# Windowed attention and a squared-ReLU MLP in one kernel: the scores of a group become one recorded operation, the planner's durations are replaced and a cost for 64/128-row changes is added, and the noise is drawn from one seed per stretch

## Chip, cores and metric

One core of one Trainium2 chip. The metric is the time of one launch in device microseconds. Three runs of the kernel before gave 292.73, 292.80 and 292.94 us (median 292.8). Engines are named as in the profile: PE is TensorE's matmuls, PEld its weight loads, DVE is VectorE, ACT is ScalarE, POOL is GpSimd, SP is SyncE.

## What is computed

```python
# q, k, v: (8, 8, 576, 64) float32; w_in: (512, 2048); w_out: (2048, 512)
scores = matmul(q, k.transpose(0, 1, 3, 2)) / sqrt(64)
scores = where(abs(pos[:, None] - pos[None, :]) <= 32, scores, -1e9)
attn = softmax(scores)
x = matmul(attn, v).transpose(0, 2, 1, 3).reshape(4608, 512)
h = maximum(x @ w_in, 0)
out = (h * h) @ w_out          # (4608, 512) float32
```

## The kernel before

All 4608 tokens pass through one pipeline. **Attention** works in 24 groups of 192 tokens (three to a batch, all 8 heads). Queries and keys of a group are loaded in bf16 by POOL's DMA queue, turned so that the 64 head dimensions lie on partitions (`turn_pe` with identity matmuls for groups 0 to 5, `turn_dma` with SP's DMA transposes after that), and multiplied: the *scores* S. Groups 3 to 23 use `scores_steps` (line 664): 24 matmuls with 64 rows of weights (two heads side by side on 128 partitions), 16 of them (steps 0 and 2, `S{G}A`) into PSUM banks 0 and 1 of the tile `at`, 8 (step 1, `S{G}B`) into banks 2 and 3. ACT takes the exponentials (`X{G}A`, tile `e`, 1024 columns, and `X{G}B`, tile `em`, 512 columns), DVE multiplies by the band mask (`M`, tile `pt`; one of 1024 columns, two of 512 on 64 partitions). Then the products with v, `pv` (line 707): two of 8 matmuls each, `P{G}A` and `P{G}B`, into banks 2 and 3 of `at`, each followed by a reciprocal `R` and a scaling `N` on DVE (tiles `xa`, `xb`); between the two the upper half of the banks is cleared (`Z`). The result is turned into `xt` (`xturn`, line 767): by PE and ACT for groups below `NXT`, by SP's DMA transposes from there on.

**The MLP** takes `xt` in tiles of 192 tokens, from token 2304 on 256 (`mm1`, line 840): calls of 8 matmuls into the banks `ht`, ReLU on ACT (tile `rt`), square on DVE or ACT (tile `gt`). The second product runs for pairs of 128-token blocks (`mm2_pair`, line 913): seven products of 8 matmuls in place of eight, with sums of `gt` blocks (`ss`) and of weights (`tw`) made on DVE; the first two blocks use `mm2`. Results leave over ACT's DMA queue.

**What sets the order.** The code records every operation with its engine, what it reads and writes, a duration and a key (a due time in units of 64 tokens). `Prog.schedule` (line 159) plays the whole program through with these durations and a latency for each engine (`LAT`): whenever an engine is free it takes, of the operations that would be ready, the one with the smallest key. Where an operation has an alternative on another engine (`FLEX`), either may take it. Keys get an offset by kind (`OFFS`) and a random part (`SEED`, `NOISE`). The order so found is written out; on the chip each engine runs its instructions in that order and waits by semaphore. In the opening, matmuls on zeros (line 386) stand where the plan has PE idle. `OPENING` is the order of the first loads, by name: `('k', 2)` are the keys of group 2, `w1` and `w2` quarters of the weights, `('v', 1, 0)` one half of the values of group 1, `hq` and `hk` the first queries and keys over SP's queue.

Of the kernel before, what the change touches and what calls it, by code (L numbers as in the profile page):

```python
# [22 lines left out]
NXT = 6  # L23
LEAD = 8
LAG = 9.0
AHEAD = 14.0
GFAR = 12
GATE = 'P{}B'
GD = 3
GK = 6.5  # L30
TDKEY = 4.5
# [14 lines left out]
NCLR = 1  # L46
# [5 lines left out]
LSLACK1 = 1000  # L52
HOLD = {}
KMIN = 0.5
HOLDT = 26000
# [8 lines left out]
SEED = 12603  # L64
NOISE = 0.2
# [7 lines left out]
OPENING = [('k', 1), ('w1', 0), ('v', 0, 0), ('q', 1), ('v', 0, 1), ('q', 2), ('k', 2), ('v', 1, 0),  # L73
# [6 lines left out]
LAGP = 9.5  # L80
PSTEP = 0.45
SLEAD = 2.0
MOE = 0.5
SQBEG = 576
ULATE = 28
HLATE = 4608
E3 = 576
E3B = 1
OFFS = {'S': 1.5, 'M': -1.0, 'g': -4.75, 'Z': -4.0, 'N': -3.75, 'cc.': 4, 'u': -2.5, 'X': 0.75, 'r': 4, 'c': -0.5}
DLEAD = 0.3  # L90
TWKEY = 5
# [3 lines left out]
FLEX = {'g': 4.75, 'Z': 0.5, 'ev': 4.5, 'o': -1.0, 'p': 3.75}  # L95
# [9 lines left out]
class Prog:  # L105
# [3 lines left out]
    LAT = {"PE": 205, "ACT": 200, "DVE": 30, "POOL": 100, "SP": 0}  # L109
# [40 lines left out]

    def free_order(self, d, op, eng):

        if d.eng == eng == "PE":
            return True
        if d in op.raw or d.dma is not None or op.dma is not None or d.eng != eng:
            return False
        return not (d in op.own and eng in ("ACT", "DVE"))

    def schedule(self):
        ops = self.ops  # L160
        rnd = random.Random(SEED)
# [17 lines left out]
        free["POOL"] = 850  # L179
        wait = {e: [] for e in engs}  # L180
# [46 lines left out]
        while True:  # L227
# [32 lines left out]
            if op.taken:  # L260
                continue
            op.eng, op.lat, op.taken = e, self.LAT[e], True
# [67 lines left out]
def act(n):  # L330
    return 52 + 0.833 * n


def dve(n, fast=True):
    return 156 + (0.525 if fast else 1.042) * n


class Gen:
# [197 lines left out]
    def turn_pe(self, t, b, g, key):  # L536
# [9 lines left out]
        def f(e):  # L546
            for j in range(4):
                for x in range(2):
# [5 lines left out]
                   dur=8 * 52, name=f"turn{t}{b}{g}")  # L554
# [44 lines left out]
    def scores(self, G, ws):  # L599
# [44 lines left out]
        self.moe = self.p.rec("PE", f, reads=rd, writes=[t for w in ws for t in tags[w]], key=key, dur=190 + 235 * len(ws),  # L644
# [19 lines left out]
    def scores_steps(self, G):  # L664
# [21 lines left out]
        self.p.rec("PE", lambda e: f(e, (0, 2)), reads=rd, writes=lo, key=key, dur=SDUR * 2 // 3, name=f"S{G}A")  # L686
# [472 lines left out]
```

## Time and profile before

| | before |
|---|---|
| median of three runs | 292.8 us |
| the profiled execution: its time, its span | 292.72 us, 290.9 us |
| granted TensorE clock | 1.0 in all 40 slices |
| busy, of the span | PE 97%, PEld 85%, ACT 75%, DVE 68%, POOL 37% |
| matmuls: pairs (256 columns) | 952 in 128x256, 273 ns each on the page |
| matmuls: scores of groups 3 to 23 | 504 in 64x64, 191 ns each on the page |

The span runs from the first to the last instruction; the 1.82 us between it and the execution's time lie around it. Matmuls are pipelined: the duration of one on the page (273 ns) is longer than the distance from its start to the next one's, so PE's busy share hides small gaps. Where the time of a piece of PE's work matters, the start of the next piece is subtracted from its own, in the view in order of time.

### The profile page before, as it was taken

How to read it: one execution, taken by the hardware profiler on the slowest of the kernel's cores; microseconds unless marked ns; L12 is line 12 of the kernel's file. 1: busy time of each engine (PE TensorE's matmuls, PEld its weight loads, DVE VectorE, ACT ScalarE, POOL GpSimd, SP SyncE). 2: the span in 40 equal slices, each digit the busy share in tenths (PEclk: the TensorE clock that was granted, in tenths of full speed). 3: DMA queues.
4: the chain of work that ended last, by engine and by line, in shares of the span. 5: the costliest groups of instructions: out<-in, count | busy, mean ns of one | idle time of the engine just before them, and what ended most of it. 6: DMA issues, size and time to landing. Idle time of an engine off the chain costs nothing.

```text
span 290.9 us, 8382 instructions
## 1 busy us (share of the span) xinstructions
PE 283.2 (97%) x3438; PEld 246.2 (85%) x3445; DVE 199.2 (68%) x433; ACT 219.4 (75%) x400; POOL 107.1 (37%) x143
## 2 busy tenths in 40 slices
PE   8898999999999999999999999999999999999996
PEld 3478788699989999999998889889888889888885
DVE  6895677885786888377847685578666877615263
ACT  4498999878858888897978776877778768676710
POOL 8999757731000245606660645216460000000000
PEclk9999999999999999999999999999999999999999
DMA  8999999999999499999999999989999230202024
GB/s 167 177 205 182 199 182 157 159 176 140 175 143 175 104 120 128 187 122 157 111 169 170 154 124 120 216 140 128 127 181 178 47 101 19 74 10 74 0 74 144
DMA packets 158151, 39.39 MB, mean 135 GB/s; under 512 B 147489, under 2 KB 153761, under 8 KB 158113
## 3 DMA queue, kind: packets, MB, share of 16 engines
q0 software_dynamic: 106016, 17.93, 86.5%
q1 hardware_dynamic: 47056, 11.88, 30.2%
q10 hardware_dynamic: 5040, 9.05, 10.2%
q8 instruction: 27, 0.44, 0.7%
q14 instruction: 12, 0.09, 0.1%
HBM read 36.70 MB, written 9.44 MB: 159 GB/s over the span
## 4 chain that ended last, share of the span: by engine, by line
PE 87%; ACT 7%; DVE 3%; DMA 2%; issue 1%; SPq 0%; ACTq 0%; DVEq 0%
PE ht L857 39%; PE outp L943 32%; PE at L943 4%; PE at L678 4%; PE at L731 4%; DMA oe<-in_k_dram 2%; PE outp L883 2%; ACT rt L863 2%; ACT e L655 1%; ACT qt L577 1%; ACT kt L582 1%; PE outp L857 1%; ACT gt L873 1%; DVE kt L580 1%; DVE qraw L493 0%
## 5 line engine op out<-in xcount | busy, mean ns | idle before, releaser
L857 PE MATMUL ht<-xt,w 128*128 128x192 bf16 (+1 forms) x1280 | 139.1, 258 | 0.0
L857 PEld LDWEIGHTS ht<-xt,w 128*128 128x128 bf16 x1280 | 112.8, 98 | 7.8
L863 ACT ACTIVATE rt<-ht 128x384 bf16<-128x384 f32 (+1 forms) x160 | 84.0, 537 | 32.8 <-PE ht L857 24.2
L873 ACT ACTIVATE gt<-rt 128x384 bf16<-128x384 bf16 (+1 forms) x122 | 69.4, 573 | 3.5 <-ACT rt L863 0.2
L507 POOL DMA_DIRECT2D v<-in_v_dram x48 | 38.3, 808 | 23.1 <-PE at L731 16.5
L458 POOL DMA_DIRECT2D kraw<-in_k_dram x36 | 28.1, 785 | 44.6 <-PE at L731 27.7
L458 POOL DMA_DIRECT2D qraw<-in_q_dram x36 | 28.2, 786 | 41.6 <-issue 34.5
L943 PE MATMUL outp<-w,gt 128*128 128x256 bf16 x240 | 31.2, 273 | 0.0
L943 PE MATMUL outp<-tw,gt 128*128 128x256 bf16 x240 | 31.1, 273 | 0.0
L943 PE MATMUL outp<-tw,ss 128*128 128x256 bf16 x240 | 30.6, 273 | 0.0
L871 DVE TENSOR_TENSOR gt<-rt 128x384 bf16<-128x384 bf16 (+1 forms) x46 | 17.2, 378 | 13.0 <-ACT rt L863 12.6
L943 PEld LDWEIGHTS outp<-tw,ss 128*128 128x128 bf16 x240 | 22.9, 98 | 2.6
L943 PEld LDWEIGHTS outp<-tw,gt 128*128 128x128 bf16 x240 | 22.9, 98 | 2.7
L943 PEld LDWEIGHTS outp<-w,gt 128*128 128x128 bf16 x240 | 22.6, 98 | 2.8
L703 DVE TENSOR_TENSOR pt<-em,mask 64x512 bf16<-64x512 bf16 x42 | 17.6, 420 | 8.8 <-ACT em L692 7.7
L689 ACT ACTIVATE e<-at 128x1024 bf16<-128x1024 f32 x21 | 21.5, 1024 | 2.2 <-PE at L678 2.0
L963 DVE TENSOR_TENSOR oe<-outp,uu 128x256 f32<-128x256 f32 (+1 forms) x30 | 16.7, 555 | 8.1 <-PE outp L943 6.9
L731 PE MATMUL at<-v,pt 128*128 128x66 bf16 x384 | 20.1, 194 | 0.5 <-ACT pt L652 0.5
L963 DVE TENSOR_TENSOR uu<-outp,uu 128x256 f32<-128x256 f32 x30 | 12.7, 422 | 10.4 <-PE outp L943 7.1
L731 PEld LDWEIGHTS at<-v,pt 128*128 128x128 bf16 x384 | 17.8, 98 | 1.8 <-ACT pt L652 0.6
L753 DVE TENSOR_TENSOR xa<-at,rs 64x512 bf16<-64x512 f32 x24 | 16.7, 695 | 1.0
L750 DVE RECIPROCAL rs<-at 64x8 f32<-64x8 f32 (+1 forms) x48 | 10.0, 208 | 10.6 <-PE at L731 9.6
(109 smaller groups left out, 324.0 us busy)
## 6 DMA issues: line engine op xcount, KB each, us to landing
out_dram<-oe ACTq DMA_DIRECT2D x34, 256.0 KB, 3.3
qraw<-in_q_dram POOLq DMA_DIRECT2D x36, 96.0 KB, 6.2
w<-in_moe_w_in_dram POOLq DMA_DIRECT2D x4, 512.0 KB, 11.1
v<-in_v_dram POOLq DMA_DIRECT2D x16, 128.0 KB, 7.8
w<-in_moe_w_out_dram POOLq DMA_DIRECT2D x4, 512.0 KB, 18.8
v<-in_v_dram POOLq DMA_DIRECT2D x16, 96.0 KB, 7.4
kraw<-in_k_dram POOLq DMA_DIRECT2D x12, 112.0 KB, 5.4
kraw<-in_k_dram POOLq DMA_DIRECT2D x12, 96.0 KB, 7.0
```

The source lines that it names most:

```text
L458: self.p.rec("POOL", lambda e, j=j: e.dma_start(raw[0:h, j, :].rearrange("p (h d) -> p h d", h=8), s[:, j]), writes=[("raw", t, G % NRAW, ...
L507: self.p.rec("POOL", lambda e, j=j, lo=lo, hi=hi, k0=k0: e.dma_start(vt[lo - k0:hi - k0, j, :, 0:64], self.v[b, :, lo:hi, :].rearrange("h ...
L689: self.p.rec("ACT", lambda e: e.activation(e2[:], self.AT[:, 0:1024], ACTF.Exp, scale=0.125), reads=lo, writes=[("e", n)], key=key, dur=ac ...
L703: self.p.rec("DVE", lambda e, w=w, r=r, x=x, mm=mm: e.tensor_tensor(pt[x:x + 64, w, :, 0:64], e1[r:r + 64, :].rearrange("p (h q) -> p h q" ...
L731: mm = e.matmul(avp[:, c:c + VS], pt[:, 4 * (h % 2) + h // 2, :], vt[:, w, h, :], start=(w == 0 and y == 0), stop=True, skip_group_check=True)
L753: self.p.rec("DVE", lambda e: e.tensor_tensor(x[r0:128, :].rearrange("p (x y c) -> p x y c", x=2, y=4), av[:, :, :, 0:64], rb, ALU.mult), ...
L857: mm = e.matmul(ht[:, n * x:n * x + n], self.W1[:, ft, 128 * d:128 * d + 128], self.XT[:, ft, r:r + n], start=(ft == 0), stop=(ft == 3))
L863: self.p.rec("ACT", lambda e: e.activation(rt[:, 0:c], ht[:, 0:c], ACTF.Relu), reads=htag, writes=[("rt", k % 4)], key=key, dur=act(c), na ...
L871: self.p.rec("DVE", lambda e: e.tensor_tensor(gt[:, d0:d0 + len(ds), r:r + n], rr, rr, ALU.mult), reads=[("rt", k % 4)], writes=wr, key=ke ...
L873: alt=("ACT", lambda e: e.activation(gt[:, d0:d0 + len(ds), r:r + n], rr, ACTF.Square), act(c), "g")
L943: mm = e.matmul(op[:, 256 * half:256 * half + 256], a[:, d, :], w[:, d, :], start=first and d == 0, stop=d == 7, skip_group_check=True)
L963: self.p.rec("DVE", lambda e: e.tensor_tensor(out, src, other, ALU.add), reads=btags[bank] + rd, writes=wr, key=key + k * PSTEP - DLEAD, d ...
```

## The change

`scores_steps` records one PE operation for the 24 score matmuls of a group. It writes all four banks and carries one semaphore count at its end; before, there were two operations with a key each.

```diff
-        self.p.rec("PE", lambda e: f(e, (0, 2)), reads=rd, writes=lo, key=key, dur=SDUR * 2 // 3, name=f"S{G}A")
-        self.moe = self.p.rec("PE", lambda e: f(e, (1,)), reads=rd, writes=hi, key=key + 0.02, dur=SDUR // 3, name=f"S{G}B")
+        if SMERGE:
+            self.moe = self.p.rec("PE", lambda e: f(e, (0, 2, 1)), reads=rd, writes=lo + hi, key=key, dur=350, name=f"S{G}B")
+        else:
...
```

The planner charges PE for a change of kind, and may hold on for a score operation that stands at most `STICK` above the smallest key:

```diff
+    def kind(self, op):
+        n = op.name
+        return "s" if n[0] == "S" or n[0] == "T" and n[-1] == "a" else "t" if n[0] == "t" else "v" if n[0] == "P" and "." not in n else ""
+
+    def change(self, a, b):
+        return 0 if a == b else 110 if b == "s" else 100 if a == "s" or b == "t" else 30 if b == "v" else 0
...
+            if e == "PE":
+                k = self.kind(op)
+                if last == "s" != k:
+                    more = [x for x in pool[e] if not x[2].taken and x[0] < first[0] + STICK and self.kind(x[2]) == "s"]
+                    if more:
+                        heapq.heappush(pool[e], (op.key, op.i, op))
+                        op = min(more)[2]
+                        k = "s"
+                t += self.change(last, k)
+                last = k
```

Durations, latencies and keys:

```diff
-    LAT = {"PE": 205, "ACT": 200, "DVE": 30, "POOL": 100, "SP": 0}
+    LAT = {"PE": 170, "ACT": 150, "DVE": 145, "POOL": 100, "SP": 0}
...
-    return 52 + 0.833 * n
+    return 60 + 0.833 * n
...
-    return 156 + (0.525 if fast else 1.042) * n
+    return (40 if fast else 60) + (0.557 if fast else 1.042) * n
...
-NXT = 6
-LEAD = 8
+NXT = 5
+LEAD = 11.0
...
-GFAR = 12
+GFAR = 10
...
-TDKEY = 4.5
+TDKEY = 3.0
...
-LAGP = 9.5
+LAGP = 7.5
...
-MOE = 0.5
+MOE = -1
...
-ULATE = 28
-HLATE = 4608
+ULATE = 32
+HLATE = 4096
...
-SEED = 12603
-NOISE = 0.2
+SEEDS = (32084, 52688, 82796, 32593, 79449, 14325, 66926, 90467, 77586, 2794, 60200, 19844, 43771, 14133, 3007, 27362, 8058, 26041, 26079, 54464)
+NOISE = 0.8
...
-            n = rnd.uniform(-NOISE, NOISE)
-            if SEED and op.key > -20:
-                op.key += n
+            if op.key > -20:
+                op.key += rnds[min(max(int((op.key + 12) // 5), 0), len(rnds) - 1)].uniform(-NOISE, NOISE)
```

Other durations are replaced in the same way (a reciprocal 117 for 212, a `turn_pe` 250 for 416, a `pv` 222 for 260, a store 420 for 600), and `OFFS`, `FLEX` and `OPENING` have new entries. The matmuls of the two products and of attention are the same in number, but for one group: with `NXT` at 5, group 5 is turned into `xt` by SP's DMA transposes (8 fewer matmuls on PE, one fewer ACT operation, two more transposes on SP). ACT has 12 squares fewer and DVE 12 more.

**PE, group 7, in the steady part.** `at<-qt,kt` are scores, `at<-v,pt` the products P, `ht<-xt,w` calls of `mm1`, `outp<-...` products of a pair. Before:

```order
L678 MATMUL at<-qt,kt 128x64 x16
L857 MATMUL ht<-xt,w 128x192 x16
L678 MATMUL at<-qt,kt 128x64 x8
L943 MATMUL outp<-tw,gt 128x256 x8
L857 MATMUL ht<-xt,w 128x192 x16
L731 MATMUL at<-v,pt 128x66 x8
L943 MATMUL outp<-w,gt 128x256 x8
L943 MATMUL outp<-w,ss 128x256 x8
L943 MATMUL outp<-tw,gt 128x256 x8
L731 MATMUL at<-v,pt 128x66 x8
```

The same group now, up to the scores of group 8:

```order
L697 MATMUL at<-qt,kt 128x64 x24
L879 MATMUL ht<-xt,w 128x192 x16
L965 MATMUL outp<-w,ss 128x256 x8
L879 MATMUL ht<-xt,w 128x192 x8
L753 MATMUL at<-v,pt 128x66 x8
L879 MATMUL ht<-xt,w 128x192 x16
L965 MATMUL outp<-tw,gt 128x256 x8
L753 MATMUL at<-v,pt 128x66 x8
L879 MATMUL ht<-xt,w 128x192 x16
L965 MATMUL outp<-w,gt 128x256 x8
L697 MATMUL at<-qt,kt 128x64 x24
```

The scores moved together. Over the program, the scores of groups 3 to 23 stood in 32 places on PE (11 of 16, 11 of 8 and 10 of 24 matmuls) and stand in 21 of 24 now.

**PE in the opening, from the first `mm1` call to the second scores of group 2.** `outp<-ident,kraw` turns the keys of group 2; `128x64 x8` from `qt,kt` with 128 columns are scores of groups 1 and 2. Before:

```order
L549 MATMUL outp<-ident,kraw 128x80 x8
L630 MATMUL at<-qt,kt 128x128 x8
L731 MATMUL at<-v,pt 128x66 x8
L857 MATMUL ht<-xt,w 128x192 x16
L630 MATMUL at<-qt,kt 128x128 x8
L857 MATMUL outp<-xt,w 128x192 x8
L731 MATMUL at<-v,pt 128x66 x8
L857 MATMUL ht<-xt,w 128x192 x8
L630 MATMUL at<-qt,kt 128x128 x8
```

Now:

```order
L649 MATMUL at<-qt,kt 128x128 x8
L879 MATMUL ht<-xt,w 128x192 x8
L753 MATMUL at<-v,pt 128x66 x8
L879 MATMUL ht<-xt,w 128x192 x8
L879 MATMUL outp<-xt,w 128x192 x8
L879 MATMUL ht<-xt,w 128x192 x8
L753 MATMUL at<-v,pt 128x66 x8
L568 MATMUL outp<-ident,kraw 128x80 x8
L833 MATMUL at<-ident,xa 128x64 x4
L649 MATMUL at<-qt,kt 128x128 x8
L838 MATMUL at<-ident,xb 128x128 x4
```

The keys of group 2 are turned later, and its first scores stand behind four `mm1` calls, not two.

**POOL's loads in the opening**, from the queries of group 1 on (`tw` is the buffer in which the first queries and keys land). Before:

```order
L490 DMA tw<-in_q_dram 96x8x128
L507 DMA v0<-in_v_dram 128x8x64
L490 DMA tw<-in_q_dram 96x8x128
L490 DMA tw<-in_k_dram 80x8x128
L507 DMA v1<-in_v_dram 64x8x64
L507 DMA v1<-in_v_dram 128x8x64
L520 DMA w1<-in_moe_w_in_dram 128x4x512 x3
```

Now:

```order
L509 DMA tw<-in_q_dram 96x8x128
L526 DMA v0<-in_v_dram 128x8x64
L526 DMA v1<-in_v_dram 64x8x64
L509 DMA tw<-in_q_dram 96x8x128
L526 DMA v1<-in_v_dram 128x8x64
L539 DMA w1<-in_moe_w_in_dram 128x4x512
L509 DMA tw<-in_k_dram 80x8x128
```

The keys of group 2 (`80x8x128`) went behind the values of group 1 and a second quarter of `w1`.

More of the change, by code (lines that the diff above doesn't have):

```diff
@@ L160, in schedule @@
         ops = self.ops
-        rnd = random.Random(SEED)
+        rnds = [random.Random(x) for x in SEEDS]
         for op in ops:
@@ L179, in schedule @@
         free["POOL"] = 850
+        last = ""
         wait = {e: [] for e in engs}
@@ L643, in scores @@
             rd += [t for w in ws for t in tags[w]]
-        self.moe = self.p.rec("PE", f, reads=rd, writes=[t for w in ws for t in tags[w]], key=key, dur=190 + 235 * len(ws),
+        self.moe = self.p.rec("PE", f, reads=rd, writes=[t for w in ws for t in tags[w]], key=key, dur=215 * len(ws),
                               name=f"S{G}{'AB'[ws[-1]]}")
@@ L741, in pv @@
             rd += [("pt", G % 2, 0, 0), ("pt", G % 2, 0, 1), ("v", G % NV, 0)]
-        self.p.rec("PE", f, reads=rd + (lo if w and G >= NDUP else []), writes=hi + lo, key=key, dur=260 + 160 * (w and G < NCLR) + 260 * (w and G < NDUP),
+        self.p.rec("PE", f, reads=rd + (lo if w and G >= NDUP else []), writes=hi + lo, key=key, dur=222 + 160 * (w and G < NCLR) + 222 * (w and G < NDUP),
                    name=f"P{G}{'AB'[w]}")
@@ L896, in mm2 @@
             self.p.rec("ACT", lambda e: e.dma_start(self.out[128 * u:128 * u + 128, :], oe),
[L897 removed]
+                       reads=[("oe", u % 4)], writes=[("out", u)], dma=(f"o{u % 4}", u), key=key, dur=420, move=(8, 80), name=f"st{u}")
     def setup_tw(self, key):
```

37 lines of the change are left out of this document (20 added, 17 removed), and 6 rows, old and new, of the table OPENING.

## The prediction, on record before the changed kernel ran

> **What bounds the kernel now.** I read the page's busy times first, then a table of stages, then PE's instructions in order of time.
>
> ```profile
> PE 283.2 (97%) x3438; PEld 246.2 (85%) x3445; DVE 199.2 (68%) x433; ACT 219.4 (75%) x400; POOL 107.1 (37%) x143
> ...
> 0.00:24.00 24.00, 20.17 (x227) 12.44 (x229) 19.38 (x60) 15.79 (x23) 23.03 (x34) 1.00 1.39 183
> 24.00:60.00 36.00, 34.83 (x460) 28.95 (x466) 25.70 (x55) 32.25 (x61) 27.24 (x36) 1.00 1.84 174
> 60.00:288.30 228.30, 228.18 (x2756) 204.78 (x2752) 153.70 (x319) 171.33 (x316) 56.83 (x74) 1.00 1.18 123
> ```
>
> The stage rows give start and end, length, the busy time of PE, PEld, DVE, ACT and POOL, the granted clock, the DMA share and GB/s. From 60 us to the end of the last matmul PE is busy 228.18 of 228.30 us at full clock; ACT has 171 and DVE 154. So in that stage the time is PE's own queue of matmuls and nothing else, and only less work on PE, or work that PE finds late, changes it. Before 24 us PE mostly fills with matmuls on zeros; from 24 to 60 us it loses little.
>
> Busy time is too coarse for the question, because a pipelined matmul lasts longer than its place in the queue. The starts tell it:
>
> ```profile
> 130.89 0.41 PE L678 MATMUL at<-qt,kt 64*128 64x64 bf16 x16
> 131.23 0.43 PE L731 MATMUL at<-v,pt 128*128 128x66 bf16 x8
> 131.50 1.48 PE L857 MATMUL ht<-xt,w 128*128 128x192 bf16 x16
> 132.82 1.04 PE L943 MATMUL outp<-w,gt 128*128 128x256 bf16 x8
> 133.69 1.04 PE L943 MATMUL outp<-tw,ss 128*128 128x256 bf16 x8
> 134.66 0.29 PE L678 MATMUL at<-qt,kt 64*128 64x64 bf16 x8
> 134.88 1.49 PE L857 MATMUL ht<-xt,w 128*128 128x192 bf16 x16
> ```
>
> Sixteen `mm1` matmuls take 131.50 to 132.82, 1.32 us, so eight take 0.66. Eight of a pair take 0.87 (132.82 to 133.69); the next eight, followed by scores, take 0.97. **Going to 64 rows costs about 0.10 us.** Sixteen scores take 0.34 and eight 0.22: eight more cost 0.12, so 0.10 of each stay is fixed. **Coming back costs about 0.10 us**, and one visit 0.20.
>
> **The change, part by part.** The sum is made against the profiled execution, 292.72 us (span 290.9, 1.82 around it), 0.08 below the median of the runs.
>
> *The merged scores.* The order has 32 visits for groups 3 to 23 before and 21 now: 11 visits less at 0.20, **-2.2 us**. All lie after 32 us, in PE's full queue, so nothing else hides them. That a merged visit costs what is assumed is in the next row group: 24 scores at 155.61 take 0.45, three times 0.12 and about 0.10.
>
> *What the merge makes later.* The exponentials now wait for all 24, and the next scores for the last reader of all four banks. The traced chain of a group that was already in one piece, `em` first on ACT:
>
> ```profile
> 155.61 0.52 PE L678 MATMUL at<-qt,kt 64*128 64x64 bf16 x24
> 156.06 1.05 PE L857 MATMUL ht<-xt,w 128*128 128x256 bf16 x8
> ...
> 156.00 0.58 ACT L692 ACTIVATE em<-at 128x512 bf16<-128x512 f32 x1
> 156.48 1.01 ACT L689 ACTIVATE e<-at 128x1024 bf16<-128x1024 f32 x1
> 157.78 0.69 DVE L697 TENSOR_TENSOR pt<-e,mask 128x1024 bf16<-128x1024 bf16 x1
> 158.69 0.42 PE L731 MATMUL at<-v,pt 128*128 128x66 bf16 x8
> 161.57 0.42 PE L731 MATMUL at<-v,pt 128*128 128x66 bf16 x8
> 163.66 0.52 PE L678 MATMUL at<-qt,kt 64*128 64x64 bf16 x24
> ```
>
> and with `e` first, so that the masks of `em` end last:
>
> ```profile
> 124.37 0.52 PE L678 MATMUL at<-qt,kt 64*128 64x64 bf16 x24
> 126.63 0.87 DVE L703 TENSOR_TENSOR pt<-em,mask 64x512 bf16<-64x512 bf16 x2
> 127.69 0.42 PE L731 MATMUL at<-v,pt 128*128 128x66 bf16 x8
> ...
> 205.06 0.52 PE L678 MATMUL at<-qt,kt 64*128 64x64 bf16 x24
> 207.97 0.87 DVE L703 TENSOR_TENSOR pt<-em,mask 64x512 bf16<-64x512 bf16 x2
> ```
>
> With `em` first the masked product is there 157.78 + 0.69 - 155.61 = 2.86 us after the scores began; with `e` first 126.63 + 0.87 - 124.37 = 3.13. PE's work between scores and first product now: for group 7 the scores, 16 and 8 of `mm1` and 8 of a pair, 0.45 + 1.32 + 0.66 + 0.87 = 3.30. Worked out in this way for all 21 groups it is 2.86 once, 3.07 five times, 3.29 to 3.30 six times and 3.47 to 4.18 nine times, and of the eight groups with `e` first on ACT seven have at least 3.47. Against these two needs, with 0.10 for the signal, PE would wait some 0.3 us in all. In the other groups that were in one piece the need was up to 3.2 with `em` first, but for one ahead of 60 us, and up to 207.97 + 0.87 - 205.06 = 3.78 with `e` first. That one, where ACT is nearly full, and the slowest reader of a second product:
>
> ```profile
> 46.54 0.52 PE L678 MATMUL at<-qt,kt 64*128 64x64 bf16 x24
> 49.34 0.67 DVE L697 TENSOR_TENSOR pt<-e,mask 128x1024 bf16<-128x1024 bf16 x1
> ...
> 133.04 0.68 DVE L753 TENSOR_TENSOR xb<-at,rs 128x512 bf16<-128x512 f32 x1
> ```
>
> It needed 3.47. At the means of the rest (2.9 and 3.5) the waits add up to 0.7 us; with every group at its top, and the two `em`-first groups ahead of 60 us at 3.47, to 3.7. I take **+0.7**, nearest the means; the ends are 0 and 3.7.
>
> The scores after the second product: 163.66 - 161.57 = 2.09 was enough above. The order leaves 1.89 three times, 2.10 once and 2.55 or more else. The slowest reader ended 133.04 + 0.68 - 131.23 = 2.49 after its product began. I take nothing, as the row of 2.09 is the nearest; if all needed 2.59, 2.7 us.
>
> The Trainium skill, "Perfetto Trace Analysis", section Optimizing Tensor Performance, speaks against this part: independent groups of matmuls should rotate through different PSUM banks, so that one is evacuated while the next computes. The row for it is the one at 130.89, where 16 scores of the next group run ahead of the second product at 131.23; that overlap is gone. By the page the sum would be that of the first rival below, and by the rows of groups in one piece, where PE did not wait, it is the sum here.
>
> *Group 5's transposes leave PE.*
>
> ```profile
> 66.96 0.29 PE L811 MATMUL at<-ident,xa 64*128 64x64 bf16 x4
> 67.18 0.40 PE L816 MATMUL at<-ident,xb 128*128 128x128 bf16 x4
> 67.41 0.82 PE L857 MATMUL ht<-xt,w 128*128 128x192 bf16 x8
> ...
> DMA to landing us min/median/max: 2.3/5.2/8.6
> ```
>
> 0.22 + 0.23 and 0.10 for going to 64 rows: **-0.55 us**. The two DMA transposes go into SP's queue among those of the queries and keys of later groups, which wait behind them. They need the 2.49 us above on DVE and 8.6 to landing, 11.1; the order has 11.2 us of PE's work between group 5's last product and the tile that reads it. I cost it at nothing; where that cover is gone, each us late is one on PE.
>
> *Twelve squares and some evictions that go from ACT to DVE*: nothing. ACT is at 75% and DVE at 68% of the span, and after 60 us PE's full queue stands above both.
>
> *The opening.*
>
> ```profile
> 6.29 0.72 POOL L490 DMA_DIRECT2D tw<-in_k_dram  x1
> 15.38 0.55 DVE L493 COPY kraw<-tw 80x1024 bf16<-80x1024 bf16 x1
> 16.98 0.91 ACT L582 ACTIVATE kt<-outp 128x640 bf16<-128x640 bf16 x1
> 18.81 0.40 PE L630 MATMUL at<-qt,kt 64*128 64x128 bf16 x8
> 24.05 0.83 PE L857 MATMUL outp<-xt,w 128*128 128x192 bf16 x8 [0.79 <-ACT rt L863]
> 33.00 0.41 PE L678 MATMUL at<-qt,kt 64*128 64x64 bf16 x16 [0.37 <-ACT kt L582]
> ...
> w<-in_moe_w_in_dram POOLq DMA_DIRECT2D x4, 512.0 KB, 11.1
> v<-in_v_dram POOLq DMA_DIRECT2D x16, 128.0 KB, 7.8
> v<-in_v_dram POOLq DMA_DIRECT2D x16, 64.0 KB, 7.6
> ```
>
> The keys of group 2 were issued at 6.29 and copied at 15.38: a queue served in its order. Now 64, 128 and 512 KB more lie ahead of them, 0.72 MB at the 183 GB/s of that stage, 3.9 us. Their eviction ended at 17.89 and the scores at 18.81 left 0.92 unused. Now two more `mm1` calls (1.32), a product (0.25) and a transpose (0.22) stand ahead of these scores, 1.8 us. So they wait 3.9 - 0.9 - 1.8 = 1.2 us, in place of the 0.79 at 24.05: **+0.4**. It may be -0.8, if the wait does not come and the 0.79 goes, or +2.2, if none of the work ahead covers it. At 33.00 the scores of group 3 waited 0.37 right behind the transposes of group 2; two `mm1` calls now stand between: **-0.4**.
>
> *The tail.* The last twelve products are the same rows in the same order: nothing.
>
> Sum: 292.72 - 2.2 - 0.55 + 0.7 + 0.4 - 0.4 = 290.67; I forecast **290.6 us**.
>
> **The rivals.**
> *One buffer is too few (slower).* The place is the wait of the first product for its mask, in each of the 21 groups. Should the need be 3.56 us throughout, the mean traced need with `e` first, and its signal, the shortfalls against 2.86 to 4.18 add up to 4.9 us: 292.72 - 2.75 + 4.9 = 294.9. It decides from a need of 3.4 us, where shortfalls equal the 2.75 saved. For it: DVE gets busier, and the old split gave slack. Against it: groups in one piece were already hidden, and `e`-first groups have the long distances.
> *The opening gives it back.* The late keys cost the full 2.2 and ReLUs pile up behind them on ACT, which is busy 32.25 of 36 us there: 290.67 + 1.8 = 292.5, no change to speak of.
> *The opening gains.* No wait for the keys, no new waits later: 292.72 - 2.75 - 0.8 - 0.4 = 288.8.
> *Transposes late.* `xt` from SP lands after its tile is due in a few groups, some 2 us: 292.7.
> *The change doesn't do what it says*: the 0.20 is not the visit's but belongs to what stands beside it, and moves along: about 292.5.
>
> **How the numbers follow.** Forecast case (289.4 to 291.6) 0.50, opening gains 0.14, opening gives it back 0.15, one buffer 0.12, transposes 0.05, no effect 0.04. The range, 288.6 to 293.7, runs from the gaining opening to the forecast's sum with 3.7 in place of its 0.7 (293.7); it leaves out most of the one-buffer case and little else. About 0.2%, 0.6 us, is what a measurement can tell from no change. Faster: 0.50 + 0.14 and 0.09 of the opening that gives back, 0.73. Same: 0.05 of that opening, the transposes' 0.03 and no effect, 0.12. Slower: the rest, 0.15.
>
> **What would show it.** In order of time: 21 pieces of 24 scores, with 0.97 for eight of a pair ahead of each and 0.45 for themselves. In the waits: first products that wait for the mask, more than 0.7 us in all, would make the one-buffer rival right. In the opening: a wait of about 1.2 us at the first scores of group 2 for their keys. After 60 us, PE's work a good 2.7 us shorter. I am wrong if PE shows new gaps after 60 us, or if the visits are as many and no cheaper.

## Result and profile after

| | before | after |
|---|---|---|
| median (lowest to highest), 6 runs each | 292.81 us (292.71 to 292.94) | 294.79 us (294.00 to 295.25) |
| the profiled execution: its time, its span | 292.72, 290.9 us | 294.93, 292.6 us |

The changed kernel is **slower**, by 0.65%: ratio 1.0065, 95% interval 1.0049 to 1.0081. The forecast was 290.6 us, with a range of 288.6 to 293.7.

The page of after and its stages, to be held against those of before (columns as there):

```profile
PE 283.8 (97%) x3442; PEld 244.6 (84%) x3442; DVE 208.2 (71%) x455; ACT 206.4 (71%) x377; POOL 107.6 (37%) x143
```

```profile
0.00:24.00 24.00, 20.62 (x224) 12.86 (x225) 16.70 (x57) 14.66 (x21) 23.03 (x35) 1.00 1.39 183
24.00:60.00 36.00, 35.12 (x475) 28.66 (x473) 28.07 (x60) 32.72 (x64) 19.89 (x26) 1.00 1.82 173
60.00:290.00 230.00, 228.02 (x2748) 203.07 (x2746) 163.15 (x340) 158.98 (x295) 64.67 (x84) 1.00 1.21 124
```

After 60 us PE was busy all but 0.12 us; now it lacks 1.98 us of 230. ACT has 12 us less work there and DVE 9 more. The chain of work that ended last, shares of the span by engine, first of before and then of after:

```profile
PE 87%; ACT 7%; DVE 3%; DMA 2%; issue 1%; SPq 0%; ACTq 0%; DVEq 0%
```

```profile
PE 73%; DVE 11%; ACT 7%; DMA 4%; issue 3%; POOL 2%; ACTq 0%; POOLq 0%; DVEq 0%
```

Work of DVE now lies on the path. The longest waits of PE after 60 us in the changed kernel, in the view in order of time (the bracket holds the idle time and who ended it):

```profile
112.76 0.43 PE L753 MATMUL at<-v,pt 128*128 128x66 bf16 x8 [0.35 <-DVE at L785]
121.39 0.83 PE L879 MATMUL ht<-xt,w 128*128 128x192 bf16 x8 [0.59 <-ACT rt L885]
143.81 1.05 PE L965 MATMUL outp<-w,ss 128*128 128x256 bf16 x8 [0.36 <-DVE oe L985]
155.19 1.05 PE L965 MATMUL outp<-w,ss 128*128 128x256 bf16 x8 [0.29 <-DVE oe L985]
```

Because matmuls overlap, the idle time is less than what is lost. So I took the start of every piece of matmuls and subtracted the work ahead of it, priced as in the prediction (192 columns 0.0825 us, 256 columns 0.109, a change of rows 0.10). Where that difference grows, PE lost time. The profiled executions, in us (one of each kernel):

| | before | after | difference |
|---|---|---|---|
| sum of the matmuls and changes of rows | 273.73 | 271.18 | -2.55 |
| lost by 60 us | 13.89 | 14.77 | +0.88 |
| lost after 60 us | 0.44 | 3.75 | +3.31 |
| the execution's time less its span | 1.82 | 2.33 | +0.51 |

These sum to 2.15, and the profiled executions differ by 2.21. After 60 us the larger pieces of the loss stand at second products (0.62), first matmuls of `mm1` calls (1.11), products of pairs (1.17) and first products (0.50).

How two of them come about in the changed kernel. At 143.81 PE waits for the bank that DVE's addition `oe` empties. DVE works without a break:

```profile
141.13 0.87 DVE L725 TENSOR_TENSOR pt<-em,mask 64x512 bf16<-64x512 bf16 x2
142.03 0.42 DVE L985 TENSOR_TENSOR uu<-outp,uu 128x256 f32<-128x256 f32 x1
142.37 0.68 DVE L951 TENSOR_TENSOR gt<-gt 128x1024 bf16<-128x1024 bf16 x1
143.09 0.21 DVE L772 RECIPROCAL rs<-at 64x8 f32<-64x8 f32 x1
143.33 0.43 DVE L985 TENSOR_TENSOR oe<-outp,uu 128x256 f32<-128x256 f32 x1
```

`oe` stands behind two masks, a sum and a reciprocal, and PE loses 0.52 us. At 121.39 PE waits for a ReLU (ACTq is a DMA issued by ACT):

```profile
117.13 0.69 DVE L719 TENSOR_TENSOR pt<-e,mask 128x1024 bf16<-128x1024 bf16 x1 [0.55 <-ACT e L711]
117.74 0.62 DVE L893 TENSOR_TENSOR gt<-rt 128x384 bf16<-128x384 bf16 x2
118.28 0.68 DVE L985 TENSOR_TENSOR oe<-outp,uu 128x512 f32<-128x512 f32 x1
118.99 1.76 ACTq L1013 DMA_DIRECT2D out_dram<-oe  x2
120.85 0.49 ACT L885 ACTIVATE rt<-ht 128x384 bf16<-128x384 f32 x1 [2.50 <-PE outp L965]
121.39 0.83 PE L879 MATMUL ht<-xt,w 128*128 128x192 bf16 x8 [0.59 <-ACT rt L885]
```

Two stores stand at the head of ACT's queue and wait for DVE's `oe`. The mask and the two squares ahead of it cost it next to nothing here: it starts 1.18 us after the product that it reads began (117.10), and in e13, where DVE stood idle for that product, 1.14. Then one store takes 1.38 us to issue. The ReLU behind them starts at 120.85 (its bracket names PE, because issuing does not count as busy), and PE's next call needs the bank that it empties. The kernel's engines take their queues in order, so one late operation holds all behind it.

The first two rows of this view show one more thing. The mask lasts 0.69 us on the page, but the next operation starts 0.61 after it. The planner of before charged 0.694 and the changed one charges 0.610: the new number is the true distance, and the old one left about 0.08 us of air behind each such operation. The Trainium skill, "Perfetto Trace Analysis", section Summary: the profiler window per engine type, states that on DVE and ACT the reported time runs to the acknowledged write and leaves out the start of the reading. That would account for a reported time that is longer than the distance of starts.

### The profile page after: what moved, and what is told of

The parts are those of the page before. It is cut to its first block, busy times and chain, and to the rows that moved or that the text cites. A ratio compares the mean times of both kernels' runs of the same rounds, so it can differ in the third digit from the quotient of the medians.

```text
span 292.6 us, 8390 instructions
## 1 busy us (share of the span) xinstructions
PE 283.8 (97%) x3442; PEld 244.6 (84%) x3442; DVE 208.2 (71%) x455; ACT 206.4 (71%) x377; POOL 107.6 (37%) x143
## 4 chain that ended last, share of the span: by engine, by line
PE 73%; DVE 11%; ACT 7%; DMA 4%; issue 3%; POOL 2%; ACTq 0%; POOLq 0%; DVEq 0%
PE ht L879 30%; PE outp L965 30%; DMA w<-in_moe_w_in_dram 4%; PE at L753 3%; ACT rt L885 3%; PE at L697 3%; PE at L879 2%; PE at L965 2%; DVE xa L775 2%; DVE ss L951 1%; ACT e L711 1%; POOL v L526 1%; DVE oe L985 1%; ACT gt L895 1%; DVE pt L725 1%
## 5 line engine op out<-in xcount | busy, mean ns | idle before, releaser
L879 PE MATMUL ht<-xt,w 128*128 128x192 bf16 (+1 forms) x1216 | 130.9, 257 | 0.7 <-ACT rt L885 0.6
L879 PEld LDWEIGHTS ht<-xt,w 128*128 128x128 bf16 x1216 | 105.7, 98 | 9.1 <-ACT rt L885 1.5
L885 ACT ACTIVATE rt<-ht 128x384 bf16<-128x384 f32 (+1 forms) x152 | 79.3, 533 | 40.5 <-PE ht L879 31.8
L895 ACT ACTIVATE gt<-rt 128x384 bf16<-128x384 bf16 (+1 forms) x110 | 62.1, 571 | 2.9
L893 DVE TENSOR_TENSOR gt<-rt 128x384 bf16<-128x384 bf16 (+1 forms) x58 | 21.9, 383 | 24.8 <-ACT rt L885 24.0
L965 PE MATMUL outp<-w,gt 128*128 128x256 bf16 x256 | 33.2, 273 | 0.0
L965 PE MATMUL outp<-tw,gt 128*128 128x256 bf16 x256 | 33.2, 273 | 0.0
L965 PEld LDWEIGHTS outp<-tw,gt 128*128 128x128 bf16 x256 | 24.7, 98 | 2.7
L719 DVE TENSOR_TENSOR pt<-e,mask 128x1024 bf16<-128x1024 bf16 x21 | 14.5, 690 | 6.0 <-ACT e L711 5.6
L965 PE MATMUL outp<-w,ss 128*128 128x256 bf16 x128 | 16.6, 273 | 0.7 <-DVE oe L985 0.7
```

The source lines that it names most:

```text
L879: mm = e.matmul(ht[:, n * x:n * x + n], self.W1[:, ft, 128 * d:128 * d + 128], self.XT[:, ft, r:r + n], start=(ft == 0), stop=(ft == 3))
L885: self.p.rec("ACT", lambda e: e.activation(rt[:, 0:c], ht[:, 0:c], ACTF.Relu), reads=htag, writes=[("rt", k % 4)], key=key, dur=act(c), na ...
L893: self.p.rec("DVE", lambda e: e.tensor_tensor(gt[:, d0:d0 + len(ds), r:r + n], rr, rr, ALU.mult), reads=[("rt", k % 4)], writes=wr, key=ke ...
L895: alt=("ACT", lambda e: e.activation(gt[:, d0:d0 + len(ds), r:r + n], rr, ACTF.Square), act(c), "g")
L965: mm = e.matmul(op[:, 256 * half:256 * half + 256], a[:, d, :], w[:, d, :], start=first and d == 0, stop=d == 7, skip_group_check=True)
```

## The experiments

"Lost" is the column of the table above; around is the median of time less span over a kernel's runs. All ratios are to the kernel before, measured beside them. "Lost" is read from one profiled execution: where two kernels have the same order on PE, ACT, DVE and SP (after and e14, e13 and e15), it differs by 0.7 and 0.9 us after 60 us, so smaller differences in that column say nothing.

| run | median us | ratio, 95% | matmul sum | lost by 60 / after 60 | around |
|---|---|---|---|---|---|
| before | 292.8 | | 273.73 | 13.89 / 0.44 | 1.81 |
| after | 294.79 | 1.0049 to 1.0081 | 271.18 | 14.77 / 3.75 | 2.34 |
| e1 | 294.30 | 1.0035 to 1.0073 | 271.18 | 14.03 / 3.46 | 2.31 |
| e2 | 296.84 | 1.0118 to 1.0159 | 272.58 | 15.07 / 4.08 | 2.03 |
| e3 | 294.00 | 1.0008 to 1.0059 | 271.38 | 15.82 / 2.49 | 2.23 |
| e4 | 296.65 | 1.0108 to 1.0161 | 271.18 | 14.42 / 6.40 | 1.85 |
| e5 | 296.32 | 1.0104 to 1.0130 | 272.73 | 14.16 / 4.54 | 1.80 |
| e6 | 297.45 | 1.0146 to 1.0195 | 272.73 | 15.15 / 4.92 | 1.83 |
| e7 | 294.12 | 1.0025 to 1.0051 | 273.93 | 13.01 / 1.48 | 1.78 |
| e8 | 298.56 | 1.0176 to 1.0202 | 271.18 | 15.91 / 5.88 | 1.95 |
| e9 | 294.37 | 1.0033 to 1.0073 | 271.93 | 13.46 / 3.25 | 1.81 |
| e10 | 291.86 | 0.9947 to 0.9980 | 271.73 | 13.96 / 1.75 | 1.82 |
| e11 | 292.08 | 0.9951 to 0.9986 | 272.93 | 12.96 / 1.34 | 1.80 |
| e12 | 294.45 | 1.0031 to 1.0064 | 271.18 | 14.18 / 3.46 | 2.05 |
| e13 | 292.31 | 0.9980 to 1.0014 | 271.18 | 14.70 / 2.04 | 1.99 |
| e14 | 294.76 | 1.0051 to 1.0094 | 271.18 | 14.36 / 4.42 | 2.13 |
| e15 | 292.93 | 0.9994 to 1.0023 | 271.18 | 14.49 / 2.96 | 1.82 |
| e16 | 292.36 | 0.9969 to 0.9999 | 271.73 | 13.59 / 1.49 | 1.80 |
| e17 | 291.71 | 0.9946 to 0.9976 | 271.73 | 13.64 / 1.21 | 1.80 |
| e18 | 291.55 | 0.9931 to 0.9969 | 271.18 | 14.34 / 1.35 | 1.99 |

### Undoing one part of the change

**e1**, the stores on SyncE, order untouched:

```diff
+        for op in self.ops:
+            if op.eng == "ACT" and op.dma is not None and op.name[:2] == "st" and op.key < 400:
+                op.eng = "SP"
```

> The changed kernel with its order untouched, except that the output stores of the loop are issued by SyncE at their place in the program and no longer by ScalarE. Theory 'in-order queues': stores at the head of ScalarE's queue wait for VectorE's copy of the product and hold the next ReLU, for which a first product of a block then waits (1.11 us of such waits after 60 us in the changed kernel). They go: 0.6 to 1.1 us less, 293.7 to 294.2 us. Theory 'VectorE alone is late' (it stands 71% busy, and the waits ascribed to the ReLU are an echo of it): no change, 294.8.

0.5 us less, just short of the forecast. The waits at 121 and 134 went, a new one of 1.07 us came at 93.47 for a ReLU behind an exponential, and those on DVE stayed as they were:

```profile
112.85 0.43 PE L756 MATMUL at<-v,pt 128*128 128x66 bf16 x8 [0.35 <-DVE at L788]
142.84 1.05 PE L968 MATMUL outp<-w,ss 128*128 128x256 bf16 x8 [0.36 <-DVE oe L988]
154.22 1.05 PE L968 MATMUL outp<-w,ss 128*128 128x256 bf16 x8 [0.29 <-DVE oe L988]
```

The stores are a part, not the whole.

**e2**, `SMERGE = False`:

> The scores of a group are two operations again, all else of the change stays (numbers, the price of a change of rows, keys, seeds). The matmuls with their changes of rows sum to 272.6 us, 1.4 more than in the changed kernel. Theory 'the merge does it' (four banks held at once, so exponentials and products of a group bunch up): waits after 60 us fall from 3.3 to at most 1 us, 293.5 to 294. Theory 'the new numbers and keys do it': the waits stay at 3 to 4 us, so 295.5 to 296.5. Theory 'the draw of seeds': anywhere between, since the order is drawn anew.

The waits stay with the merge undone, and the time rises by more than the matmuls, to a little above the highest forecast. So the merge is not needed to make such waits.

**e3**, the old durations and latencies (the three that matter most):

```diff
-    LAT = {"PE": 170, "ACT": 150, "DVE": 145, "POOL": 100, "SP": 0}
+    LAT = {"PE": 205, "ACT": 200, "DVE": 30, "POOL": 100, "SP": 0}
...
-    return (40 if fast else 60) + (0.557 if fast else 1.042) * n
+    return 156 + (0.525 if fast else 1.042) * n
...
-                       reads=[("oe", u % 4)], writes=[("out", u)], dma=(f"o{u % 4}", u), key=key, dur=420, move=(8, 80), name=f"st{u}")
+                       reads=[("oe", u % 4)], writes=[("out", u)], dma=(f"o{u % 4}", u), key=key, dur=600, move=(8, 80), name=f"st{u}")
```

> Planned durations and latencies as before (VectorE 156 ns base and not 40, a store 600 ns and not 420, ScalarE's latency 200 and not 150), all else of the change stays. Matmul sum 271.4. Theory 'the longer planned durations were slack that kept ScalarE and VectorE ahead of TensorE': waits after 60 us fall from 3.3 to under 1.5, and the time to 292.0 to 293.2. Theory 'keys and seeds do it': waits stay at 3 or more, 294.5 to 296. Theory 'merge': the same, 294.5 to 296.

2.49 lost after 60 us in place of 3.75, and 0.8 us less in the median: the right direction, but between the two forecasts.

**e4**, the old keys (`OFFS`, `FLEX`, `NOISE = 0.2`, `LEAD`, `LAGP` and others):

> The keys of before (offsets by kind, price of a change of engine, noise 0.2 and not 0.8, lags and leads), with the merged scores, the new durations and the price of a change of rows. Matmul sum 271.2 as in the changed kernel. Theory 'keys and noise put VectorE's and ScalarE's operations in a bad order': waits after 60 us fall under 1.5, 292.0 to 293.2. Theory 'new durations': waits stay at 3 or more, 294.5 to 296.

Worse, 6.40, and above both forecasts. The new keys are not the fault by themselves. But each of e2 to e4 also draws the whole order anew, and the next pair of seeds shows what a draw is worth.

**e7**, the kernel before with `SEED = 777`, and **e8**, the changed kernel with other `SEEDS`:

> The kernel before with another seed (777) for the noise on its keys and nothing else; matmul sum 273.93, 0.2 more. Theory 'luck of the draw' (an order drawn anew costs some us of small waits on VectorE and ScalarE, and the order of before was a good draw): waits after 60 us of 2 us and more instead of 0.4, 295 to 298. Theory 'the numbers and keys of the change are what removed the slack': an order drawn with the old numbers stays within 1 us, 292.5 to 294.

> The changed kernel with other seeds per stretch and nothing else; matmul sum 271.2, as in the changed kernel. Theory 'luck of the draw': somewhere between 293 and 298, with the waits at other places than in the changed kernel. Theory 'the merge or the new numbers make the waits': they stay near 3 to 4 us after 60 us, of the same kinds, 294 to 296.

A new seed costs the old planner 1.2 us and the new one 3.8. e7 lies between its two forecasts and e8 above all of its own. Two draws are no distribution, but a draw is worth as much as the effects sought, so the runs that follow hold an order fixed or choose it on purpose.

### The merge alone, in the order of before

**e5** and **e6** keep the order of before and join the halves in groups 3, 7, 8, 17 and 19, where block products stand between (a and z are the two halves, q is PE's order; e5 has the first pair of lines, e6 the second):

```diff
+            q.remove(a)
+            q.insert(q.index(z), a)
...
+            q.remove(z)
+            q.insert(q.index(a) + 1, z)
```

> The kernel before with its planned order kept on every engine, except that in five groups (3, 7, 8, 17, 19), where a few block products stand between the two halves of the scores on TensorE, the first half is moved down to just ahead of the second. Five changes to 64 rows and back go, the matmul sum falls from 273.73 to 272.73. Theory 'the price of 0.20 us a visit is right and merging alone costs nothing': 0.8 to 1.1 us less than before, 291.7 to 292.1. Theory 'the merge itself makes waits' (the first exponential starts 0.7 to 1.7 us later in each of the five groups, and products wait for its mask): no gain or up to 1.5 us more, 292.6 to 294.3.

> As the run before, but in the same five groups the second half is moved up to just behind the first, so that no exponential is later; the second half then needs its two banks 0.7 to 1.7 us sooner. Matmul sum 272.73. Theory 'merging alone costs nothing': 291.7 to 292.1. Theory 'four banks at once are the price': TensorE waits up to 1 us in each of the groups for the copies that clear the banks, 292.6 to 295.

Each edit saves 1.0 us of matmuls and loses over 4; both times lie 2 us and more above the highest forecast. The waits of e5, then of e6, in order of time:

```profile
78.68 1.49 PE L896 MATMUL ht<-xt,w 128*128 128x192 bf16 x16 [0.41 <-ACT rt L902]
80.51 0.41 PE L770 MATMUL at<-v,pt 128*128 128x66 bf16 x8 [0.33 <-issue]
89.54 1.05 PE L982 MATMUL outp<-w,gt 128*128 128x256 bf16 x8 [1.21 <-DVE uu L1002]
...
200.10 1.05 PE L896 MATMUL ht<-xt,w 128*128 128x256 bf16 x8 [0.51 <-ACT rt L902]
201.70 0.43 PE L770 MATMUL at<-v,pt 128*128 128x66 bf16 x8 [0.55 <-DVE pt L742]
```

```profile
77.53 0.29 PE L717 MATMUL at<-qt,kt 64*128 64x64 bf16 x8 [0.69 <-DVE xb L792]
86.63 0.29 PE L717 MATMUL at<-qt,kt 64*128 64x64 bf16 x8 [1.72 <-DVE xb L792]
...
175.84 0.29 PE L717 MATMUL at<-qt,kt 64*128 64x64 bf16 x8 [0.33 <-DVE xb L792]
199.35 0.29 PE L717 MATMUL at<-qt,kt 64*128 64x64 bf16 x8 [1.11 <-DVE xb L792]
```

In e6 the second half waits for the banks in all four groups after 60 us, until DVE's `xb` has read the product of the group ahead. That agrees with the Trainium skill, "Perfetto Trace Analysis", section Optimizing Tensor Performance, by which independent groups should rotate through PSUM banks. In e5 only the products at 80.51 and 201.70 are first products of the merged groups. The other three wait for ReLUs and for a sum of DVE: a later exponential pushes back what stands behind it on ACT's and DVE's queues, and matmuls that have nothing to do with attention wait. **In an order made for two halves the split is worth more than its visit**; whether merging pays depends on the order around it.

### Slack

For e9 to e13 and e16 an order was chosen by replaying it: each engine takes its planned queue in order, with every operation as long as traced; in a second form ACT's and DVE's operations are late by a random time up to 0.1 us. The replay only chooses the order; every time here is measured.

**e9** and **e10** have the merged scores, the traced durations, and the keys, loads and `NXT = 6` of before. In both, as in e11 and e12, the scores also wait for all halves of their turned queries and keys. e9's seeds and a few of its keys were chosen for little wait in the exact replay, e10's in the one with lateness. The latencies of e9, then of e10:

```diff
+    LAT = {"PE": 150, "ACT": 180, "DVE": 155, "POOL": 100, "SP": 0}
...
+    LAT = {"PE": 170, "ACT": 240, "DVE": 195, "POOL": 100, "SP": 0}
```

> Merged scores, price of a change, a seed per stretch and the traced durations, but the keys and the order of loads of before; seeds and small keys were chosen so that the plan, replayed with every operation exactly as long as traced, shows TensorE almost no wait after 60 us (0.24 us). Matmul sum 271.9. Theory 'no slack' (an operation of ScalarE or VectorE that ends up to 0.1 us late finds nothing between it and TensorE): the chip makes 3 to 5 us of waits of it all the same, as in the changed kernel, 293 to 295. Theory 'keys and the order of loads of the change were the fault': waits under 1 us, 290.0 to 291.0.

> The same parts as in the run before (merged scores, price of a change, traced durations, keys and loads of before), but planned with 90 and 50 ns more latency on ScalarE and VectorE, and its seeds chosen so that the replayed plan waits little when each of their operations is late by a random time up to 0.1 us. Replayed exactly it waits 0.36 us, no less than the run before. Matmul sum 271.7. Theory 'no slack': waits after 60 us under 1.5 us, 289.5 to 291.0, faster than the kernel before. Theory 'merged scores cost their waits in any order' or 'luck of the draw': 293 to 295, like the run before.

2.5 us apart, and e10 is faster than before, though 0.9 us above the top of its forecast. After 60 us the profiles differ by 1.50 us (3.25 and 1.75). Another 0.9 us lies behind the start of PE's last piece, where e9's last pieces stand in another order. The ends of e9 and of e10:

```profile
287.76 1.04 PE L965 MATMUL at<-tw,gt 128*128 128x256 bf16 x8
...
288.84 0.69 DVE L985 TENSOR_TENSOR oe<-at,e 128x512 f32<-128x512 f32 x1 [1.87 <-PE at L965]
289.56 0.42 DVE L978 COPY oe<-at 128x256 f32<-128x256 f32 x1
```

```profile
286.57 1.04 PE L965 MATMUL at<-w,gt 128*128 128x256 bf16 x8
...
286.77 0.69 DVE L985 TENSOR_TENSOR oe<-at,e 128x512 f32<-128x512 f32 x1 [0.98 <-PE at L965]
287.71 0.42 DVE L978 COPY oe<-at 128x256 f32<-128x256 f32 x1 [0.25 <-PE at L965]
```

In e10 the long addition of DVE runs beside the last matmuls; in e9 it comes after them, with the copy behind it: the copy starts 1.80 us after the last piece and not 1.14, which is 0.66 of the 0.9. So of e9's 2.5 us about 1.5 speak for slack, in one pair of orders.

**e11**, as e10 with the scores in two operations (and 20 ns more per operation of DVE and on ACT's latency):

> As the run before, planned and chosen in the same way and with the same effort, but with the scores of a group as two operations, which the order again parts in some groups. Matmul sum 272.9. Theory 'no slack, and the merge is worth a little once the order has slack': waits under 1.5 us, 290.3 to 291.8, 0.3 to 1.2 above the run before. Theory 'the merge is the fault': at least 1.5 us below the run before.

292.08 against 291.86: with slack in both, 1.2 us fewer matmuls leave 0.2 that their spreads (291.15 to 293.57, e10 290.68 to 292.79) can't tell from nothing. Neither forecast of this run holds fully; in these two orders the merge is no fault, and it brings no gain that shows.

**e12**, the changed kernel with latencies of 200 and 195 ns and seeds chosen with lateness:

> The changed kernel with all its parts and its keys, loads and noise, planned with 50 ns more latency on ScalarE and VectorE, its seeds chosen for small lateness as in the two runs before. Matmul sum 271.2. Theory 'no slack': waits after 60 us of 1 to 2.5 us, 289.8 to 291.8, 3 to 5 us below the changed kernel. Theory 'keys and loads of the change are the fault': 293.5 to 295.5.

A miss for slack: 294.45, in the range of the rival that blames keys and loads, and 3.46 us lost after 60 us, spread over many waits of 0.1 to 0.3. Its last pieces stand as in e9, which accounts for some 0.9. Latency and seeds alone didn't make an order with slack out of the new keys. e4, which has the old keys and lost 6.40, speaks against blaming the new ones alone; this is not settled.

### The queues behind PE's order

**e13** keeps the changed kernel's order on PE, POOL and SP and makes 95 moves by one to three places on ACT and DVE:

```diff
+MOVES = (("DVE", 132, 134), ("DVE", 372, 375), ("ACT", 101, 102),
...
+        for e, i, j in MOVES:
+            seqs[e].insert(j, seqs[e].pop(i))
```

> The changed kernel with TensorE's, GpSimd's and SyncE's order exactly as it is; 95 moves by one to three places on ScalarE's and VectorE's queues after 55 us, chosen so that the replayed order waits little when their operations are late by a random time up to 0.1 us. Matmul sum 271.2, the merged scores and every count of instructions stay. Theory 'only the order of the two queues is at fault': waits after 60 us fall from 3.3 to 0.8 to 1.8 us, 292.2 to 293.4. Theory 'TensorE's own order asks too early (merged scores, new keys)': waits stay at 2.5 us or more, 294 to 295.

**2.5 us less with the same matmuls in the same order**, level with the kernel before. Of this 0.35 is time around the span; in the profiles the loss after 60 us falls by 1.71, and that at products of pairs from 1.17 to 0.12. The place of 143.81 in this run:

```profile
141.63 0.42 DVE L1017 TENSOR_TENSOR oe<-outp,uu 128x256 f32<-128x256 f32 x1
...
142.08 0.21 DVE L804 RECIPROCAL rs<-at 64x8 f32<-64x8 f32 x1
142.32 0.42 DVE L757 TENSOR_TENSOR pt<-em,mask 64x512 bf16<-64x512 bf16 x1
142.37 1.04 PE L997 MATMUL outp<-w,ss 128*128 128x256 bf16 x8
```

The reciprocal and one of the two masks now stand behind `oe`, and the product follows its call without a wait. The place of 121.39:

```profile
118.54 0.69 DVE L1017 TENSOR_TENSOR oe<-outp,uu 128x512 f32<-128x512 f32 x1 [0.35 <-PE outp L997]
...
119.27 0.82 ACTq L1045 DMA_DIRECT2D out_dram<-oe  x2
...
120.93 0.82 PE L911 MATMUL ht<-xt,w 128*128 128x192 bf16 x8
```

Here the call no longer waits because the stores take 0.82 us and not 1.76, which no move made.

**e14**, the changed kernel with eight more instructions on POOL (16 waits in the code, 202 instructions and not 194 in the profile), **e15**, e13 with the same, and **e16**, e10 with 14 moves on ACT and DVE:

```diff
+            if op.eng == "POOL":
+                npool += 1
+                for _ in range(16 if npool == 100 else 0):
+                    e.wait_ge(sems["PE"], 1)
```

> The changed kernel with eight more instructions on GpSimd in the middle of the program (waits on a semaphore value long reached) and nothing else. Theory 'a load of instructions after the end': with 202 instructions on GpSimd that load comes during the span and hides, the time around the span falls from 2.34 to about 1.8 us, 294.2 to 294.4 us at a span of 292.5. Theory 'the two only go together by chance': the load after the end stays, 294.8.

> Both edits: the moves on ScalarE's and VectorE's queues and eight more instructions on GpSimd. If both theories hold, 0.5 us below the run with the moves alone, 291.7 to 292.9, and faster than the kernel before or level with it; if only the moves count, as that run.

> The order with slack (merged scores, traced durations with 90 and 50 ns more latency, keys and loads of before) with 14 moves by one to three places on ScalarE's and VectorE's queues; TensorE's order untouched. The replay with lateness gives 0.25 us less wait than without the moves. Theory 'order of the two queues': 291.4 to 291.8, 0.1 to 0.5 us below that order's 291.86. Theory 'what is left are stalls that no order of these queues removes': 291.7 to 292.1.

The time around the span falls by 0.21 (2.34 to 2.13) and 0.17 (1.99 to 1.82), less than the 0.5 forecast. The whole does not follow: e14 has the changed kernel's median, its span 0.1 to 0.2 longer, and e15 is 0.6 above e13. e14 is also the changed kernel's order once more. The three longest waits on DVE come again, at 113.71, 144.05 and 155.43 with 0.35, 0.36 and 0.29 us idle; the call at 121.39 has none, and in its stead a product at 74.01 waits 0.88 for a clear on ACT behind a store that took 2.11 us. So most of the waits belong to the order, and those behind slow stores change from one execution to the next. e16 is 0.5 above e10, not below; with both spreads over 2 us, moves that the replay holds worth 0.25 don't show.

**e17** is e10 and **e18** is e13, with the edit of e1:

> The order with slack, its output stores in the loop issued by SyncE at their place and no longer by ScalarE. Theory 'slow issues of stores are the lateness that the slack is for': 0.3 to 0.8 us less than that order's 291.86, 291.0 to 291.6. Rival 'with slack they no longer reach TensorE': no change, 291.6 to 292.2. Rival 'SyncE's own transposes are held instead': 292.5 or more.

> The changed kernel with its ScalarE and VectorE queues nudged, and the output stores in the loop issued by SyncE. Theory 'slow issues of stores': 0.3 to 0.8 us less than the nudged order's 292.31, 291.5 to 292.0. Rival 'with slack they no longer reach TensorE': 292.1 to 292.6, since its profile has no wait left that a store made.

e18 is 0.8 below e13 and has the lowest median of all, **0.5% below the kernel before**; e17 gains 0.15, within its spread, as the rival that slack hides the stores has it. The place of 121.39 in e18:

```profile
118.25 0.81 SPq L1048 DMA_DIRECT2D out_dram<-oe  x2
...
119.06 0.49 ACT L920 ACTIVATE rt<-ht 128x384 bf16<-128x384 f32 x1 [1.14 <-PE ht L914]
...
119.99 0.82 PE L914 MATMUL ht<-xt,w 128*128 128x192 bf16 x8
```

The ReLU waits for PE's product and no longer for a store. The spread is small too: 291.27 to 291.98, where e13 ranged from 291.94 to 294.86.

## Why the prediction was wrong

- **The merged scores, -2.2, and group 5's transposes, -0.55**: right within 0.2. There are 30 visits of 64 rows in all and no longer 41, group 5's transposes among them (one score operation of the opening stands apart that did not before): 10 x 0.20 + 0.55 = 2.55. The prices hold, since the sums made with them leave only 0.44 us in 228 in the kernel before. No call after 60 us waited for a transposed tile.
- **First products that wait for their mask, +0.7**: 0.50 after 60 us. Right, with the size near the means; no row stands beside its 0.10 for the signal, and the three products that waited here start 0.05 to 0.14 us after the end of their mask. The first rival ("one buffer is too few") had its sign right and its place wrong: it put the whole loss here.
- **Scores after the second product, nothing**: right in this order (0.08). e6 shows what it costs where the order leaves no room: 4.5 us at four groups.
- **Squares and evictions from ACT to DVE, "nothing ... after 60 us PE's full queue stands above both"**: this step failed. A share of 71% says nothing of when an operation is done. The prediction followed two kinds of waits, because only there did PE's order change, and let the order of ACT's and DVE's queues pass at no cost, although all of it was planned anew. Second products (0.62) and products of pairs (1.17) came to wait for places in DVE's queue, `mm1` calls (1.11) for ReLUs behind stores in ACT's, 2.9 us that had no term; 0.76 of it is the one call behind a slow store. e13 shows that the two queues make a large part: with PE's order unchanged, moves on ACT and DVE lower the median by 2.5 us and the loss after 60 us from 3.75 to 2.04, and e18, with the stores off ACT's queue, to 1.35. Which part the twelve squares have was not tried by itself.
- **The table of durations had no term either.** It takes about 0.08 us of air from each operation of DVE and 180 ns from each store. This is air between the operations of a queue: as DVE's latency goes from 30 to 145, the result of a mask is planned later than before, at 610 + 145 and not 694 + 30 ns. e3 gives 0.8 us back with the old numbers; e9 against e10 shows that an order which waits little by exact times loses 3.25 us on the chip, and one chosen with lateness 1.75, but e12, chosen with lateness too, loses 3.46. That the air was what kept the order of before whole is made likely by e3 and e10, not shown: each of them is another order.
- **The opening, +0.4 and -0.4**: 0.88 by 60 us in this execution; e1, e13, e14, e15 and e18 have the same order there and lost 0.1 to 0.8 more than before. (The matmuls on zeros take 6.3 of PE's 20.17 busy us before 24 us, which is not most of it.) The late keys made no wait of their own: they landed at 19.71 and not 14.37, and DVE copied them from 19.83, straight behind a square. These waits came:

```profile
19.22 0.83 PE L879 MATMUL outp<-xt,w 128*128 128x192 bf16 x8 [0.62 <-DMA w<-in_moe_w_in_dram]
22.00 0.29 PE L833 MATMUL at<-ident,xa 64*128 64x64 bf16 x4 [0.74 <-DVE xb L775]
24.94 0.83 PE L879 MATMUL outp<-xt,w 128*128 128x192 bf16 x8 [0.23 <-ACT rt L885]
```

The first is for the second quarter of `w1`. It was issued earlier than before (7.79 and not 8.55) and landed later (19.18 and not 18.84). But the order of loads did not fix that: in e13, with the same loads, the quarter landed at 17.14 and the wait is gone. PE still stood 0.77 us for `xb` at 22.00, and the scores of group 2 began at 22.33, here at 22.34. So the places of the operations on ACT and DVE set the time there too, which the prediction did not follow.
- **The time around the span was taken as fixed at 1.82**: it is 2.28 to 2.35 in the runs of the changed kernel, +0.5.
- **The tail, nothing**: right for this kernel; e9 shows that another order of the last pieces costs 0.9.

What stays open: what made the order of ACT's and DVE's queues worse (durations, keys or the draw, which e3, e4 and e8 change each with a new order), why e12 kept its waits, 0.3 of the 0.5 us around the span, and how much of the 3.3 us a typical draw would lose rather than this one.

## What to carry to other kernels

When an order is planned anew, follow every queue that feeds the full engine, not only the instructions that the change names: an engine at 70% still holds the bound engine where an operation stands behind a late one. Exact durations make a tighter plan, not a safer one; judging an order by what it loses when operations come some 0.1 us late helped in one of two kernels here (e10, not e12). And consider keeping operations with a long tail of durations, here the stores, off a queue on which the bound engine waits: it gave 0.5 and 0.8 us in two orders and nothing that shows in the third.

## What the hardware showed unasked

**Issuing a store has a long tail.** In the 17 profiles with the loop's stores on ACT (511 of them after 60 us) 56 took more than 0.6 us, 1 to 5 a profile and up to 2.40; the rest are at 0.34 to 0.6. Two stores from one place of the same order, of e15 and of e13:

```profile
100.51 1.62 ACTq L1049 DMA_DIRECT2D out_dram<-oe  x1
```

```profile
100.89 0.36 ACTq L1045 DMA_DIRECT2D out_dram<-oe  x1
```

Of the 56 slow ones 44 ran beside a DMA transpose being issued by SP, of the others 266 of 455. The Trainium skill, "Perfetto Trace Analysis", section DMA Instruction — HWDGE (DVE, Sync), says that two engines share a generator of descriptors and that the wait for its lock lies in the reported time, which would fit; these counts alone don't show it, since a longer store meets more transposes.

**Instructions may be loaded after the last one.** In the window from 290 us on, the changed kernel shows this queue, and e14 doesn't:

```profile
q14 instruction: 1, 0.01, 0.4%
```

Eight kernels have 191 to 194 instructions on POOL (after, e1, e2, e3, e8, e12, e13, e18) and 1.95 to 2.34 us around the span. Seven of them have this load after the end of the span; e8 has it 1.75 us ahead of its end. Those with 198 or more have none and 1.78 to 1.85, but for two: e14 keeps 2.13 without it, and e17, whose SP has 30 instructions more, shows such a load and 1.80. With the eight added instructions e14 and e15 have no such load and 0.2 us less. e14's other 0.3 is not explained, and e8 shows that a load after the end is not the whole cause.
